# Attention with two feed-forward layers on one core: the high halves of k copied by GpSimd, and all pieces that prepare the next head pairs placed anew

## The chip, the core and the metric

The kernel runs on one core of one Trainium2 chip. Five engines run beside each other, each through its own instructions in a fixed order: TensorE (PE: matrix products and transposes, with its weight loads as PEld), VectorE (DVE), ScalarE (ACT), GpSimd (POOL), and SyncE (SP), which here only issues DMAs. ScalarE issues some DMAs too; these stand in its instruction order. Waits between engines go by semaphores. The metric is the device time of one execution in microseconds (us); lower is better.

## The reference

```python
q_pool = q.reshape(B, H, S // 2, 2, D).mean(axis=3)      # B=2, H=8, S=1152, D=64
scores = matmul(q_pool, k.T) / sqrt(D)                   # 576 x 1152 for each batch and head
attn = exp(scores - max(scores)); attn /= sum(attn) + 1e-9
x = matmul(attn, v)                                      # as 1152 tokens x 512
xn = x / sqrt(mean(x * x) + 1e-6) * rms_g
y = (silu(xn @ w_gate) * (xn @ w_val)) @ w_out           # 512 -> 1536 -> 512
h = y @ w_in2                                            # 512 -> 2048
out = (h * tanh(softplus(h))) @ w_out2                   # 2048 -> 512
```

All is float32. The kernel holds an operand of a product as a sum of two float16 numbers, a high half (the value rounded to float16) and a low half (what the rounding left), and adds the three products high-high, high-low and low-high.

## The kernel before

The 16 heads are worked on as 8 pairs of heads (the code's `g`, 0 to 7). A pair has 9 steps (its `j`): in each, 128 rows of pooled q of one head meet all 1152 keys; the last step of a pair takes 64 rows of both heads. So there are 72 steps, `n` from 0 to 71, and n mod 9 is called the step's place below, 0 to 8. The rest of the program (about 407 of the span's 657 us) is the feed-forward part.

`attn_step(n)` writes down the instructions of one step; they run in that order on each engine:

- TensorE: the scores of step n (six products of 128 x 384, tile `s` in PSUM; two buffers in turn); up to eight transposes of k and q halves for the next pair, where the step has them, into the first bank of the other score buffer; three transposes of the exponentials of step n-1 (tile `ep`, which has one buffer); the products of step n-5 with v (27 of them; 54 at the step that holds both heads).
- ScalarE: the high halves of the exponentials of step n-1 (`hl`, L296), those of the part transposed on TensorE (`et`, L323), a square for the RMS norm where one is due, a copy for the next pair where the plan has one (`kv_hi`, `q_hi`: tiles `khl`, `qhl`, `vv`), and the exponential of step n (`e`, L283), which needs the row maximum.
- VectorE: the row maximum of step n (L274), the copy of finished transposes to SBUF (`kqT`, L209), the low halves of `et` (L138), every few steps the division of finished rows of attention (`r`, `x`), and last the piece of `scale` that the plan has (`kv_scale`, `q_scale`: a multiplication by 64 in place, L145 and L174).
- GpSimd: the low halves of the exponentials of step n-1 (`hl`, L138: input minus high half), and the pieces of `pool` that the plan has (`kv_lo`, `q_add`, `q_lo`).

Before a pair begins, its k, q and v have to be loaded, multiplied by 64, split into halves and, for k and q, transposed. These pieces are spread over the steps of earlier pairs by the table `PLAN`: an entry (t, what) of an engine stands at step 9g + t for the pair g that it prepares. `FIRST` has other places for pair 1. `each(n, engine)` walks the table, and within a step the pieces of a smaller t's pair may come behind or ahead by the loop order.

A few buffers tie the pieces together. The loaded k and v lie in four buffers in turn (`nat`), so that a load waits for the low half of the tile that stood there; the halves of k (`khl`), those of q (`qhl`) and the sum of q's pairs (`qs`) have one buffer each; the exponentials (`e`) have three, the halves `hl` four, and `et` five. From step 42 the RMS norm of the first batch is worked in (every fourth step an `xn`, L537, on VectorE, with its halves `xh` on ScalarE and GpSimd), and from step 59 the first weight tiles (`gx`, `c`, `stretch`).

Of the kernel before, what the change touches and what calls it, by code (L numbers as in the profile page):

```python
# [41 lines left out]
def kernel(  # L42
# [13 lines left out]
    nc = tc.nc  # L56
    B, H, S, D = q.shape
# [15 lines left out]
    NTI = 2 * NI + 1  # L73
    NPR = B * NP
# [38 lines left out]
    nat, kqT, vvt, cvt = {}, {}, {}, {}  # L113
# [33 lines left out]
    def kv_hi(w, g, e):  # L147
        if e == 0:
            if w == "k":
                cvt["k", g] = cv_p.tile([128, 2 * NJ, 2 * D], F16, tag="khl", name="khl")  # L150
            else:
                t = kq_p.tile([128, 2 * NJ, 2 * D + 2], F16, tag="vv", name="vv")
                nc.gpsimd.memset(t[:, :, 2 * D:2 * D + 1], 1.0)
                vvt[g] = t
        t = (cvt["k", g] if w == "k" else vvt[g])[:, e * NJ:(e + 1) * NJ, :]
        o = 0 if w == "k" else D
        sc = 1.0 if g else QK_S if w == "k" else V_S
        nc.scalar.activation(out=t[:, :, o:o + D], in_=nat[w, g, e], func=ACTF.Copy, scale=sc)

    def kv_lo(w, g, e):  # L160
# [50 lines left out]
    def kq_first():  # L211

        t = kqT[0] = kq_p.tile([128, 2 * NJ + 2 * NTI, 128], F16, tag="kqT", name="kqT")
        for s0, n in ((2 * NJ, 2 * NTI), (0, 2 * NJ)):
            e = 0 if s0 else 1
            kv_hi("v", 0, e)
            kv_lo("v", 0, e)
            ps = s_buf[e].bitcast(F16)
            for s in range(s0, s0 + n):
                w, z = divmod(s - 2 * NJ, NTI)  # L220
                if s < 2 * NJ:
                    src = cvt["k", 0][:, s, :]
                else:
                    src = cvt["q", 0][:, z, w:w + 2, :].rearrange("p t d -> p (t d)")
                c, o = divmod(s - s0, 8)
                nc.tensor.transpose(out=ps[:, c, o * 128:(o + 1) * 128], in_=src, identity=ident)
            for c in range(-(-n // 8)):
                z = min(8, n - 8 * c)
                o = t[:, s0 + 8 * c:s0 + 8 * c + z, :]
                i = ps[:, c, 0:z * 128].rearrange("p (s t) -> p s t", s=z)  # L230
                if c == 1:
                    nc.vector.tensor_copy(out=o, in_=i)
                else:
                    nc.scalar.activation(out=o, in_=i, func=ACTF.Copy)
# [465 lines left out]
    def o_part(c, t, part, parts):  # L700
# [13 lines left out]
        if part == parts - 1:  # L714
            o = ot_p.tile([128, DM], F32, tag="ot", name="ot")
            nc.scalar.activation(out=o, in_=ps, func=ACTF.Copy, scale=1.0 / (G_S * W_S))
            for p0, p1, dst in out_rows(T):
# [4 lines left out]


    PLAN = {
        "load": [(-17, load, "k", 0), (-16, load, "k", 1), (-12, load, "q", 0), (-11, load, "q", 1), (-10, load, "q", 2),
                 (-9, load, "v", 0), (-5, load, "v", 1)],
        "act": [(-12, kv_hi, "k", 0), (-10, kv_hi, "k", 1), (-6, q_hi, 0), (-5, q_hi, 1), (-4, kv_hi, "v", 0),
                (1, kv_hi, "v", 1)],
        "scale": [(-13, kv_scale, "k", 0), (-11, kv_scale, "k", 1), (-7, q_scale), (-5, kv_scale, "v", 0),
                  (0, kv_scale, "v", 1)],  # L730
        "pool": [(-11, kv_lo, "k", 0), (-9, kv_lo, "k", 1), (-8, q_add), (-6, q_lo), (-3, kv_lo, "v", 0),
                 (2, kv_lo, "v", 1)],
        "flip": [(-9, 0), (-7, 1), (-4, 2), (-2, 3), (-1, 4)],
    }

    FIRST = {
        "load": {}, "act": {-12: -8, -10: -7}, "scale": {-13: -9, -11: -8}, "pool": {-11: -7, -9: -6},
        "flip": {-9: -6, -7: -5},
    }

    def each(n, engine):

        for t, *what in PLAN[engine]:
            for g in range(1, NPR):
                at = NTI * g + (FIRST[engine].get(t, t) if g == 1 else t)
                if at != n:
                    continue
                if engine == "flip":
                    yield g, FL[what[0]]
                else:  # L750
                    f, *a = what
                    f(*([a[0], g, a[1]] if f in (load, kv_hi, kv_lo, kv_scale) else [g, *a]))

    def do(n, engine):
        for _ in each(n, engine):
            pass

    def attn_step(n):
        scores(n)
        turns = list(each(n, "flip"))  # L760
        for g, f in turns:
            kq_flip(read[n - 1], g, *f)
        flip_pe(n - 1)
        split_hi(n - 1)
        if n:
            split_lo(n - 1)
            flip(n - 1)
        part_hi(n - 1)
        x_sums(1)
        do(n, "act")  # L770
        row_max(n)
        for g, f in turns:
            kq_keep(n - 1, g, f[0])
        part_lo(n - 1)
        row_exp(n)
        do(n, "pool")
        do(n, "load")
        if n >= LAG:
            attn_v(n - LAG)
            attn_r(n - LAG)  # L780
            attn_x(n - LAG)
        do(n, "scale")
        read.pop(n - 1, None)

    with tc.manual_schedule():
# [69 lines left out]
        for step in TAIL:  # L855
# [5 lines left out]
            else:  # L861
                n = NIT - LAG + int(step)
# [114 lines left out]
```

## Time and profile before

| | |
|---|---|
| Median of 3 runs | 658.35 us (657.65 to 659.39) |
| The profiled execution | 659.05 us, of which the span is 657.3 us |
| Steps 0 to 71 (first exponential to last) | 16.9 to 245.7 us |
| PE, DVE, ACT, POOL busy over the span | 91%, 63%, 60%, 47% |

The page of the profile gives busy time by engine and by line; the timelines give single instructions with their start and length, and in brackets how long the engine had been idle and what released it. A view by windows gives the busy time of each engine between two moments. An interval below is the time from one start of the exponential to the next: it is the length of a step on ScalarE.

### The profile page before, as it was taken

The numbers are of one execution on the slowest core, as the hardware profiler recorded it, in microseconds if no ns is written. First come the engines' busy times: TensorE is split into PE (matmuls) and PEld (weight loads), VectorE is DVE, ScalarE is ACT, GpSimd is POOL, SyncE is SP. The second block draws the span as 40 slices with busy tenths as digits, with TensorE's granted clock in tenths as the row PEclk, the third lists the DMA queues.
The fourth block names the chain that finished last, engine by engine and source line by source line (L and its number), as shares of the span: only waits on it lengthen the run. The fifth ranks groups of instructions, "written<-read, shape, count | busy, mean of one in ns | idle before, by whom it ended". The sixth has DMA issues, their size and how long they took to land.

```text
span 657.3 us, 14631 instructions
## 1 busy us (share of the span) xinstructions
PE 597.6 (91%) x5880; PEld 419.1 (64%) x5880; DVE 413.2 (63%) x679; ACT 391.7 (60%) x661; POOL 309.9 (47%) x255
## 2 busy tenths in 40 slices
PE   3588989887887789899999999999999999999997
PEld 2366767666656567677777777777655555555553
DVE  4798989889998896568888311554499931111110
ACT  4799999998987886666666331442455533223221
POOL 0778988878896861567778420441233310000000
PEclk9899999999998999999999999999999999999999
DMA  6599999998999996545556202453244100001001
GB/s 195 133 184 202 203 192 186 210 194 183 174 209 217 181 177 143 145 145 176 172 183 192 65 1 65 130 184 105 85 140 153 41 17 32 1 2 48 1 1 48
DMA packets 161908, 84.05 MB, mean 128 GB/s; under 512 B 124720, under 2 KB 152368, under 8 KB 161840
## 3 DMA queue, kind: packets, MB, share of 16 engines
q1 hardware_dynamic: 151184, 67.71, 46.8%
q10 hardware_dynamic: 10656, 15.40, 7.8%
q8 instruction: 46, 0.75, 0.5%
q14 instruction: 22, 0.18, 0.1%
HBM read 50.07 MB, written 2.36 MB: 80 GB/s over the span
## 4 chain that ended last, share of the span: by engine, by line
PE 65%; ACT 14%; DVE 8%; issue 8%; POOL 2%; ACTq 1%; DMA 1%; DVEq 0%; POOLq 0%
ACT e L283 6%; PE z L576 5%; PE z L578 5%; PE z L577 5%; PE po L713 5%; PE po L712 5%; PE po L711 5%; PE pg L576 3%; PE pv L578 3%; PE pg L577 3%; PE pv L576 3%; PE pv L577 3%; PE pg L578 3%; PE py L576 3%; PE py L578 3%
## 5 line engine op out<-in xcount | busy, mean ns | idle before, releaser
L138 POOL TENSOR_TENSOR hl<-e,hl 128x768 f16<-128x768 f32 x71 | 117.9, 1663 | 55.8 <-ACT hl L296 26.8
L274 DVE CUSTOM_DVE_ANT_1 junk<-s,shift 128x1152 bf16<-128x1152 f32 x72 | 97.2, 1351 | 8.1 <-PE s L255 7.5
L283 ACT ACTIVATE e<-s,m 128x1152 f32<-128x1152 f32 x72 | 87.6, 1217 | 13.6 <-DVE m L274 12.8
L255 PE MATMUL s<-kqT 128*128 128x384 f16 (+1 forms) x480 | 85.4, 333 | 10.2 <-DVE kqT L209 8.1
L140 DVE SCALAR_TENSOR_TENSOR g<-mo,g 128x384 f16<-128x384 f32 x48 | 26.8, 562 | 93.3 <-ACT g L686 93.3
L138 POOL TENSOR_TENSOR stretch<-c,stretch 128x512 f16<-128x512 f32 x40 | 47.8, 1194 | 60.6 <-ACT stretch L451 60.3
L347 PE MATMUL av<-vv,et 128*128 128x65 f16 (+1 forms) x720 | 74.1, 193 | 0.9 <-DVE x L395 0.9
L349 PE MATMUL av<-vv,et 128*128 128x64 f16 (+1 forms) x720 | 74.0, 193 | 0.0
L350 PE MATMUL av<-vv,et 128*128 128x65 f16 (+1 forms) x720 | 73.9, 195 | 0.0
L347 PEld LDWEIGHTS <-et 128*128 128x128 f16 (+1 forms) x720 | 67.2, 101 | 2.4 <-issue 2.3
L349 PEld LDWEIGHTS <-et 128*128 128x128 f16 (+1 forms) x720 | 67.0, 100 | 0.7
L350 PEld LDWEIGHTS <-et 128*128 128x128 f16 (+1 forms) x720 | 67.1, 100 | 0.0
L434 DVE TENSOR_SCALAR c<-raw 128x512 int32<-128x512 int32 x68 | 48.2, 708 | 26.6 <-POOL woh L138 24.5
L138 POOL TENSOR_TENSOR h<-fo,h 128x288 f16<-128x288 f32 x48 | 45.0, 937 | 42.0 <-ACT h L613 42.0
L296 ACT ACTIVATE hl<-e 128x768 f16<-128x768 f32 x72 | 60.6, 842 | 3.9 <-POOL khl L138 1.8
L576 PE MATMUL z<-y,w2i 128*128 128x384 f16 x192 | 62.6, 326 | 0.0
L577 PE MATMUL z<-y,w2i 128*128 128x384 f16 x192 | 62.6, 326 | 0.0
L578 PE MATMUL z<-y,w2i 128*128 128x384 f16 x192 | 62.6, 326 | 0.0
L680 ACT ACTIVATE mo<-z 128x384 f32<-128x384 f32 x48 | 23.2, 484 | 64.1 <-PE z L578 63.9
L444 DVE SCALAR_TENSOR_TENSOR c<-gx,c 128x512 int32<-128x512 int32 x52 | 57.7, 1110 | 4.1 <-ACT gx L424 2.2
L255 PEld LDWEIGHTS <-kqT 128*128 128x128 f16 (+1 forms) x480 | 39.7, 101 | 31.7 <-issue 13.5
L576 PE MATMUL pg<-stretch 128*128 128x288 f16 x192 | 54.9, 286 | 2.1 <-DMA stretch<-xh 1.6
(110 smaller groups left out, 1549.1 us busy)
## 6 DMA issues: line engine op xcount, KB each, us to landing
raw<-in_moe_w_out_dram SPq DMA_DIRECT2D x28, 512.0 KB, 3.4
raw<-in_moe_w_in_dram SPq DMA_DIRECT2D x16, 512.0 KB, 3.9
raw<-in_moe_w_gate_dram SPq DMA_DIRECT2D x8, 512.0 KB, 3.5
raw<-in_moe_w_val_dram SPq DMA_DIRECT2D x8, 512.0 KB, 3.8
vn<-in_v_dram ACTq DMA_DIRECT2D x14, 288.0 KB, 4.4
kn<-in_k_dram ACTq DMA_DIRECT2D x12, 288.0 KB, 4.1
qn<-in_q_dram ACTq DMA_DIRECT2D x12, 256.0 KB, 3.8
raw<-in_moe_w_gate_dram ACTq DMA_DIRECT2D x4, 512.0 KB, 4.7
```

Of the source, the lines that this page charges most:

```text
L138: eng.tensor_tensor(out=out_, in0=in_, in1=hi, op=ALU.subtract)
L255: mm = nc.tensor.matmul(out=ps[p0:p0 + m, c, 0:SN], lhsT=qt[:, w * NTI + slot, p0:p0 + m], rhs=kt[:, e * NJ + c * per:e * NJ + (c + 1) * p ...
L274: nc.vector.tensor_tensor_reduce(out=junk.rearrange("p (c s) -> p c s", c=SC), in0=ps[:, :, 0:SN], in1=shift.unsqueeze(2).to_broadcast([12 ...
L283: nc.scalar.activation(out=e.rearrange("p (c s) -> p c s", c=SC), in_=ps[:, :, 0:SN], func=ACTF.Exp, bias=m, scale=s_scale)
L296: nc.scalar.activation(out=t[:, 0, :], in_=e_t[n][:, 0:NB * 128], func=ACTF.Copy)
L347: nc.tensor.matmul(out=av[0:m, o0:o0 + D + 1], lhsT=hi, rhs=vr[:, D:2 * D + 1], start=(jj == 0), stop=False)
L349: nc.tensor.matmul(out=av[0:m, o0:o0 + D], lhsT=hi, rhs=vr[:, 0:D], start=False, stop=False)
L350: nc.tensor.matmul(out=av[0:m, o0:o0 + D + 1], lhsT=et[:, z + (NB if jj < NB else PB), p0:p0 + m], rhs=vr[:, D:2 * D + 1], start=False, st ...
L444: nc.vector.scalar_tensor_tensor(out=c, in0=g, scalar=3, in1=c, op0=ALU.logical_shift_left, op1=ALU.bitwise_or)
L576: nc.tensor.matmul(out=ps, lhsT=w0, rhs=x0, start=(i == 0), stop=False)
L577: nc.tensor.matmul(out=ps, lhsT=w0, rhs=x1, start=False, stop=False)
L578: nc.tensor.matmul(out=ps, lhsT=w1, rhs=x0, start=False, stop=(i == n - 1))
```

## The change

The high halves of k for the pairs 2 to 7 are copied by `tensor_copy` on GpSimd instead of an activation on ScalarE; pairs 0 and 1 keep ScalarE. The plan is written anew: k is loaded, multiplied and split one step earlier, the pieces on ScalarE are left with q at t = -6 and -4 and v at -2 and 1, both low halves of v stand within their own pair at t = 1 and 2, and the multiplication of v's first half moves from t = -5 to -3. The transposes stay. `FIRST` becomes a full table for pair 1.

```diff
         o = 0 if w == "k" else D
         sc = 1.0 if g else QK_S if w == "k" else V_S
+        if w == "k" and g > 1:
+            nc.gpsimd.tensor_copy(out=t[:, :, o:o + D], in_=nat[w, g, e])
+            return
         nc.scalar.activation(out=t[:, :, o:o + D], in_=nat[w, g, e], func=ACTF.Copy, scale=sc)
...
     PLAN = {
-        "load": [(-17, load, "k", 0), (-16, load, "k", 1), (-12, load, "q", 0), (-11, load, "q", 1), (-10, load, "q", 2),
-                 (-9, load, "v", 0), (-5, load, "v", 1)],
-        "act": [(-12, kv_hi, "k", 0), (-10, kv_hi, "k", 1), (-6, q_hi, 0), (-5, q_hi, 1), (-4, kv_hi, "v", 0),
-                (1, kv_hi, "v", 1)],
-        "scale": [(-13, kv_scale, "k", 0), (-11, kv_scale, "k", 1), (-7, q_scale), (-5, kv_scale, "v", 0),
+        "load": [(-18, load, "k", 0), (-17, load, "k", 1), (-14, load, "q", 0), (-13, load, "q", 1), (-12, load, "q", 2),
+                 (-7, load, "v", 0), (-6, load, "v", 1)],
+        "act": [(-6, q_hi, 0), (-4, q_hi, 1), (-2, kv_hi, "v", 0), (1, kv_hi, "v", 1)],
+        "scale": [(-14, kv_scale, "k", 0), (-12, kv_scale, "k", 1), (-8, q_scale), (-3, kv_scale, "v", 0),
                   (0, kv_scale, "v", 1)],
-        "pool": [(-11, kv_lo, "k", 0), (-9, kv_lo, "k", 1), (-8, q_add), (-6, q_lo), (-3, kv_lo, "v", 0),
-                 (2, kv_lo, "v", 1)],
+        "pool": [(-13, kv_hi, "k", 0), (-12, kv_lo, "k", 0), (-11, kv_hi, "k", 1), (-10, kv_lo, "k", 1), (-9, q_add),
+                 (-6, q_lo), (1, kv_lo, "v", 0), (2, kv_lo, "v", 1)],
         "flip": [(-9, 0), (-7, 1), (-4, 2), (-2, 3), (-1, 4)],
     }
-    FIRST = {
-        "load": {}, "act": {-12: -8, -10: -7}, "scale": {-13: -9, -11: -8}, "pool": {-11: -7, -9: -6},
-        "flip": {-9: -6, -7: -5},
-    }
+    FIRST = dict(
+        PLAN,
+        act=[(-8, kv_hi, "k", 0), (-7, kv_hi, "k", 1), (-5, q_hi, 0)] + PLAN["act"][1:],
+        scale=[(-9, kv_scale, "k", 0), (-8, kv_scale, "k", 1), (-7, q_scale)] + PLAN["scale"][3:],
+        pool=[(-9, q_add), (-7, kv_lo, "k", 0), (-6, kv_lo, "k", 1), (-5, q_lo)] + PLAN["pool"][6:],
+        flip=[(-6, 0), (-5, 1)] + PLAN["flip"][2:],
+    )
     def each(n, engine):
-        for t, *what in PLAN[engine]:
-            for g in range(1, NPR):
-                at = NTI * g + (FIRST[engine].get(t, t) if g == 1 else t)
-                if at != n:
+        for g in range(1, NPR):
+            for t, *what in (PLAN if g > 1 else FIRST)[engine]:
+                if NTI * g + t != n:
                     continue
```

Three places show the order before and now. The first is VectorE in steps 14 to 16 (places 5 to 7), before; `junk, m` is the row maximum that opens a step, `kn` a loaded half of k multiplied by 64.

```order
L209 COPY kqT<-s 128x1024
L138 TENSOR_TENSOR et<-ep,et 128x384
L145 TENSOR_SCALAR kn<-kn 128x2x288
L274 ISA junk,m<-s,shift 128x1152
L274 ISA m 128x1
L138 TENSOR_TENSOR et<-ep,et 128x384
```

The same stretch of VectorE now, from the copy of step 14 to the row maximum of step 16; `vn` is the first half of v of pair 2, `kn` the second half of k of pair 3.

```order
L212 COPY kqT<-s 128x1024
L138 TENSOR_TENSOR et<-ep,et 128x384
L277 ISA junk,m<-s,shift 128x1152
L277 ISA m 128x1
L138 TENSOR_TENSOR et<-ep,et 128x384
L145 TENSOR_SCALAR vn<-vn 128x2x288
L145 TENSOR_SCALAR kn<-kn 128x2x288
L277 ISA junk,m<-s,shift 128x1152
```

Before, place 5 ended in one multiplication and place 6 in none; now place 5 has none and place 6 has two in a row, and the next row maximum stands behind both. This is so at place 6 of each of the pairs 0 to 5.

The second place is GpSimd in steps 13 to 18, before: the low halves of the exponentials, and between them the constant column of v (`MEMSET`) and the low halves of v and k.

```order
L138 TENSOR_TENSOR hl<-e,hl 128x768 x2
L153 MEMSET vv 128x18
L138 TENSOR_TENSOR hl<-e,hl 128x768
L138 TENSOR_TENSOR vv<-vn,vv 128x9x64
L138 TENSOR_TENSOR hl<-e,hl 128x768
L138 TENSOR_TENSOR khl<-kn,khl 128x9x64
L138 TENSOR_TENSOR hl<-e,hl 128x768 x2
L138 TENSOR_TENSOR khl<-kn,khl 128x9x64
```

GpSimd in the same steps now; `CAST` is the copy of k's high half.

```order
L138 TENSOR_TENSOR hl<-e,hl 128x768 x2
L159 CAST khl<-kn 128x9x64
L138 TENSOR_TENSOR hl<-e,hl 128x768
L138 TENSOR_TENSOR khl<-kn,khl 128x9x64
L138 TENSOR_TENSOR hl<-e,hl 128x768
L153 MEMSET vv 128x18
L159 CAST khl<-kn 128x9x64
L138 TENSOR_TENSOR hl<-e,hl 128x768
L138 TENSOR_TENSOR khl<-kn,khl 128x9x64
```

At place 6 (step 15) the low half of k's first tile now follows that of the exponentials; before, it was the low half of v. Each step from place 5 round to place 3 now has a piece on GpSimd beside the low half of the exponentials, and place 4 has none.

The third place is VectorE where the RMS norm is worked in, in step 54 (place 0) of the kernel now; `xn` is the normalised row, L540 there.

```order
L212 COPY kqT<-s 128x1024
L138 TENSOR_TENSOR et<-ep,et 128x384
L145 TENSOR_SCALAR vn<-vn 128x2x288
L540 SCALAR_TENSOR_TENSOR xn<-x,w_2312,gbc 128x512
L277 ISA junk,m<-s,shift 128x1152
```

That stretch reads alike before; of the other steps with an `xn`, step 50 before had a multiplication of k in front of it and step 58 one of v, both of which are gone from there now, while step 46 now has that of q.

## Rows read from the trace of the kernel before

**Rows 1.** Windows (pairs 0, 2, 6): length; busy of PE, PEld, DVE, ACT, POOL; PEclk; DMA.
```profile
16.93:46.90 29.97, 21.46 (x258) 15.14 (x259) 24.71 (x41) 25.62 (x34) 21.66 (x16) 0.89 0.77 154
...
73.88:100.64 26.76, 23.89 (x400) 18.43 (x397) 24.36 (x47) 25.24 (x34) 22.90 (x17) 1.00 1.10 201
...
186.11:219.93 33.82, 26.05 (x401) 19.70 (x397) 31.09 (x50) 26.59 (x36) 25.99 (x19) 0.95 0.97 199
```

**Rows 2.** Timeline of ScalarE, pair 2: start, length, line, tiles, [idle before, released by].
```profile
76.83 1.21 ACT L283 ACTIVATE e<-s,m 128x1152 f32<-128x1152 f32 x1
...
82.63 1.22 ACT L283 ACTIVATE e<-s,m 128x1152 f32<-128x1152 f32 x1
...
88.18 0.49 ACT L323 ACTIVATE et<-ep 128x384 f16<-128x384 f32 x1 [0.51 <-PE ep L318]
...
89.14 1.21 ACT L283 ACTIVATE e<-s,m 128x1152 f32<-128x1152 f32 x1
90.39 0.85 ACT L296 ACTIVATE hl<-e 128x768 f16<-128x768 f32 x1
91.14 0.47 ACT L323 ACTIVATE et<-ep 128x384 f16<-128x384 f32 x1
91.51 0.67 ACT L158 ACTIVATE khl<-kn 128x576 f16<-128x576 f32 x1
...
92.08 1.21 ACT L283 ACTIVATE e<-s,m 128x1152 f32<-128x1152 f32 x1
...
94.71 1.22 ACT L283 ACTIVATE e<-s,m 128x1152 f32<-128x1152 f32 x1
...
97.86 1.21 ACT L283 ACTIVATE e<-s,m 128x1152 f32<-128x1152 f32 x1
...
100.64 1.22 ACT L283 ACTIVATE e<-s,m 128x1152 f32<-128x1152 f32 x1
```

**Rows 3.** Timeline of GpSimd, steps 24 and 25.
```profile
91.37 1.65 POOL L138 TENSOR_TENSOR hl<-e,hl 128x768 f16<-128x768 f32 x1 [1.85 <-issue]
...
94.30 1.65 POOL L138 TENSOR_TENSOR hl<-e,hl 128x768 f16<-128x768 f32 x1
```

**Rows 4.** Timeline of VectorE, steps 23 to 26.
```profile
89.75 0.45 DVE L145 TENSOR_SCALAR kn<-kn 128x576 f32<-128x576 f32 x1
...
95.32 0.95 DVE L145 TENSOR_SCALAR kn<-kn 128x576 f32<-128x576 f32 x1
96.25 1.36 DVE L274 CUSTOM_DVE_ANT_1 junk<-s,shift 128x1152 bf16<-128x1152 f32 x1
...
99.17 1.36 DVE L274 CUSTOM_DVE_ANT_1 junk<-s,shift 128x1152 bf16<-128x1152 f32 x1
```

**Rows 5.** Timeline of VectorE, step 54.
```profile
187.00 0.60 DVE L145 TENSOR_SCALAR vn<-vn 128x576 f32<-128x576 f32 x1
187.52 1.77 DVE L537 SCALAR_TENSOR_TENSOR xn<-x,w,gbc 128x512 f32<-128x512 f32 x1
```

**Rows 6.** Timeline of GpSimd, steps 54 and 55.
```profile
187.25 1.49 POOL L138 TENSOR_TENSOR khl<-kn,khl 128x576 f16<-128x576 f32 x1
188.71 2.08 POOL L138 TENSOR_TENSOR hl<-e,hl 128x768 f16<-128x768 f32 x1
```

**Rows 7.** Timeline of ScalarE, steps 58 and 59.
```profile
199.48 1.21 ACT L283 ACTIVATE e<-s,m 128x1152 f32<-128x1152 f32 x1
...
205.63 1.22 ACT L283 ACTIVATE e<-s,m 128x1152 f32<-128x1152 f32 x1 [2.48 <-DVE m L274]
```

**Rows 8.** Timeline of VectorE, step 58.
```profile
200.81 1.40 DVE L145 TENSOR_SCALAR vn<-vn 128x576 f32<-128x576 f32 x1
202.13 2.13 DVE L537 SCALAR_TENSOR_TENSOR xn<-x,w,gbc 128x512 f32<-128x512 f32 x1
```

**Rows 9.** Instructions on tile khl: count, ns min/median/max, first and last start.
```profile
L138 POOL TENSOR_TENSOR khl<-kn,khl x14: 1279/1505/1512, 23.9 to 187.2; 128x576 f16<-128x576 f32 x14
```

**Rows 10.** Groups of GpSimd: busy us, mean ns, idle before.
```profile
masks.py:199 POOL TENSOR_SCALAR_AFFINE_SELECT ident<-ident 128x128 f16<-128x128 f16 x1 | 0.3, 295 | 0.1
```

## The prediction, made before the kernel ran

> **What bounds the kernel now.** I read the windows of the attention part by pairs first, then the timelines of ScalarE, VectorE and GpSimd over one pair, since a table of places can only be judged step by step. In pair 2, which has nothing but attention in it, four engines are nearly full: of 26.76 us ScalarE is busy 25.24, VectorE 24.36, TensorE 23.89 and GpSimd 22.90 [rows 1]. So the reader should not look for the one engine that bounds, but at each place for the last wait. ScalarE alone sets the least length of a step: from an exponential's start to that of `hl` 1.25 us (90.39 less 89.14), to `et` 0.75 more, to the next piece 0.37, together 2.37; a copy for the next pair adds 0.57 (92.08 less 91.51) [rows 2].
>
> Two waits lengthen that. One is TensorE's: at place 4 `et` waited 0.51 us for the transposes behind the products of the step with both heads [rows 2]. The other is between VectorE and GpSimd. A multiplication on VectorE takes 0.45 us while GpSimd rests, but 0.95 when it starts at 95.32 while GpSimd's low half of 94.30 runs until 95.95: it ends 0.32 after that [rows 3, 4]. Two such operations in a row are worse. In step 54 `vn` was directly followed by `xn` on VectorE; GpSimd's next instruction started in between (187.25), and `xn` took 1.77 us, ending 0.55 after GpSimd's end at 188.74 [rows 5, 6]. In step 58 the same couple took 1.40 and 2.13, and the exponential waited 2.48 us for its row maximum in an interval of 6.15 us [rows 7, 8]. The second of two such operations waits for a whole instruction of GpSimd.
>
> **The change part by part**, for a pair of the middle (intervals by place, before from [rows 2]).
>
> Place 5 loses k's copy on ScalarE: 2.94 becomes 2.37, -0.57. Place 7 loses the other: 3.15 becomes about 2.6, -0.55. With ScalarE shorter, place 8 is left with VectorE's own work, 2.92 from one row maximum to the next (96.25 to 99.17 [rows 4]) against 2.78 before, +0.14. Places 3 and 4 together took 6.51 (82.63 to 89.14); a q copy leaves place 4, but TensorE's chain through 54 products stands there, so 0. Place 0 keeps 2.95.
>
> Places 1 and 2 took 5.80 (76.83 to 82.63). q's multiplication moves from place 2 to place 1, where it meets GpSimd's low half again: that runs until about 1.5 after the exponential's start (below), the multiplication ends 0.32 later, the row maximum starts 0.08 before that, and the exponential 1.45 after the row maximum (from 99.17 to 100.64 it was 1.47 [rows 2, 4]): about 3.2. Place 2 has a q copy and 2.37 + 0.57 = 2.94. Sum 6.1, +0.3.
>
> Place 6 is where two multiplications now stand in a row, with nothing between them. GpSimd's low half starts 0.13 after `hl` ends (91.37 against 91.24) and lasts 1.65 [rows 2, 3], so it ends 1.25 + 0.85 + 0.13 + 1.65 = 3.88 after the exponential of place 5, which is 1.51 after that of place 6. The first multiplication arrives within it and ends at 1.51 + 0.32 = 1.83. GpSimd's next instruction, k's low half, is ready (its high half was made a step before) and goes in between: 1.28 undisturbed [rows 9], 1.49 with a VectorE operation ahead of it [rows 6], from 1.47 to 2.96. The second multiplication ends at 3.28, the row maximum starts at 3.20, the exponential at 4.65. Before it was 2.63: +2.0. Queued behind the second multiplication on VectorE are that row maximum, and behind it the exponential, everything on ScalarE, and TensorE's transposes.
>
> One pair: -0.57 - 0.55 + 0.14 + 0.3 + 2.0 = +1.3 us; pairs 1 to 3 make +3.9.
>
> The new instruction, the copy on GpSimd, is not in the trace. Below it is a one-input operation of 128 elements at 0.295 us [rows 10], above it the two-input operation of its own shape at 1.28 [rows 9]. I take 0.9, nearer to the latter. At place 5 it lies in a gap (GpSimd sat idle 1.85 us before 91.37 [rows 3]), and no multiplication stands in place 5 or 7; only in the steps with norms would 1.3 instead of 0.9 show, with +0.8 in all.
>
> There one may weigh a rule that speaks against the change. The Trainium skill (Perfetto Trace Analysis, Optimizing Scalar/DVE Operations) reminds that GpSimd reads SBUF by a port of VectorE's, so that work put on one may hold up the other. By that rule twelve copies of 0.9 would take up to 11 us out of VectorE; by the places none meets a VectorE multiplication, and the sum takes nothing for it. No run here shows the copy yet.
>
> Pair 0: place 6 with +2.0, places 5, 7 and 8 with -1.0, and q's low half one step later behind a low half of the exponentials, for which transposes wait, +0.5. The loads of v now wait on ScalarE for k's low halves in steps 2 and 3 (before, one load of k did), and `hl` queues behind each; TensorE's transposes wait for the same low halves, so I add nothing. Together +1.5, between +0.5 and +3. Pairs 4 and 5: squares on ScalarE already lengthen places 3 and 5, so GpSimd's low half ends earlier against the exponential and place 6 costs about 1.4; with the copies gone from ScalarE the rest nearly pays for it: +0.2 each. Pair 6: step 58 loses its `vn` in front of `xn`, and 6.15 [rows 7] becomes place 4's usual 3.6 (6.51 less some 2.9 for place 3) plus 1.0 for an `xn` that waits once, 4.6: -1.55. v's multiplication stands in step 60 instead, in front of an operation on the first weights, +1.4 as in pairs 4 and 5; step 61 gains about 1.3, the length of v's low half (the shape of [rows 9]), which GpSimd has no longer in front of it; place 3 gains 0.57, places 0 to 2 lose 0.3. Sum about -1.8; these are estimates. Pair 7: +0.1.
>
> All: 1.5 + 3.9 + 0.4 - 1.8 + 0.1 = +4.1 us, on a path that ends with the attention part; the feed-forward part behind it starts later by as much and is not changed. The profiled execution took 659.05 us and would take 663.15; the median of the runs lies 0.7 below that execution, so 658.35 + 4.1 = 662.4 us.
>
> **The rivals.** First, VectorE may start its second multiplication before GpSimd's waiting instruction gets in; the two of place 6 then cost 0.37 more (0.45 less the 0.08 of overlap), the place is 3.5 instead of 4.65, and in pairs 0 to 4 that takes off about 1.1 each. 4.1 - 5.5 = -1.4: 657.0 us, not slower. For it: the two rows of before have an `xn`, another operation, second. Against it: GpSimd's instruction stands ready in both, and got in both times. It decides from the length of the second `kn` at place 6: 0.4 or 1.5.
>
> The Trainium skill (SBUF — State Buffer, Who interferes with whom) has a rule for just this: the pair of ports common to VectorE and GpSimd is locked by the instruction that issues first, for its whole length, whichever engine that is. Issue order would give this rival if VectorE's second operation came first; by the rows GpSimd's came first, and the trace agrees with the rule (1.77 and 2.13 us for the second).
>
> Second, the granted clock. It was 0.89 over pair 0, where TensorE waits for the first k and q, and 0.95 over pair 6 with its long interval, and 1.00 in pair 2 [rows 1]; 0.05 of 33.82 us is 1.7 us of clock lost, as 3.4 us at the lower of the two levels (1.2 instead of 2.4 GHz) would lose it. The hole of 2.0 us at place 6 comes six times; if the clock falls each time and half of it reaches the path, that is +5: 667.4 us. Against it: pair 6, with an interval of 6.15 us [rows 7], shows no more than that.
>
> Third, ScalarE, the fullest engine of pair 2, may be the bound after all: twelve copies of 0.57 leave it, 6.8 us, and if the longer waits on VectorE lie beside TensorE's products the kernel takes 651.5 us. Against it: VectorE has 24.36 of 26.76 us already, and its waits come out of that remainder.
>
> **How the numbers follow.** Forecast 0.63, first rival 0.17, second 0.12, third 0.08. I count a difference of over 0.3% (2.0 us) as told apart from no change. Slower: all but a little of the forecast and the second rival, 0.74. Within 0.3%: most of the first rival and the low edge of the forecast, 0.14. Faster: the third and a quarter of the first, 0.12. The forecast's own range is 660 to 665, from pair 0's bounds, the copy's, and +1.0 to +1.5 for a middle pair. The whole range is 656.8 to 667.0: it holds the first rival and nearly the second, and leaves out the third.
>
> **What would show it.** Right: in steps 6, 15, 24, 33, 42 and 51 `vn` at about 1.2 us and `kn` behind it at about 1.5, GpSimd's k low half between, and an exponential that waits over 1 us for its row maximum; a pair 2 of about 28.0 us; intervals of 2.4 at places 3 and 5; step 58 near 4.6. Wrong: `kn` at 0.45 behind `vn`; copies on GpSimd over 1.3 us that push its low halves into later steps; a granted clock below 1.00 in pairs 1 to 5; or a feed-forward part of another length than before.

## The result: 9.4 us slower, more than twice the forecast

The changed kernel took 668.3 us (median of 4 runs, 666.88 to 668.68), the kernel before 658.87 us (4 runs, 657.65 to 660.75): the ratio is 1.0141, 95% interval 1.0117 to 1.0165. The forecast was 662.4 us with 667.0 as its upper end. The sign was right, and so was the wait that it named. Two losses that it had not counted make up most of the rest: one operation of VectorE that GpSimd held up in pair 7, and stretches at the lower level of TensorE's clock.

**The profile after.** The profiled execution took 668.59 us with a span of 666.8 us, 9.5 us more than before. The feed-forward part behind the last exponential is as long as it was: 255.25 to 666.8 us is 411.5 us, and before 245.71 to 657.3 was 411.6. So all of it lies in the attention part. First the windows of pairs 0, 2, 6 and 7 and of single steps (17, 56, 15 and 66; columns as in [rows 1]; pair 7 to the start of its last exponential).

```profile
17.27:48.75 31.48, 23.01 (x263) 15.90 (x262) 25.63 (x41) 24.89 (x32) 21.82 (x17) 0.86 0.78 148
78.21:105.89 27.68, 24.18 (x407) 18.82 (x404) 25.35 (x47) 24.22 (x32) 22.91 (x19) 1.00 1.06 186
193.25:225.93 32.68, 26.14 (x401) 19.84 (x397) 28.74 (x50) 26.81 (x36) 24.50 (x18) 0.95 1.14 211
225.93:255.25 29.32, 22.36 (x365) 16.69 (x363) 24.64 (x42) 22.93 (x32) 20.16 (x14) 0.94 0.99 158
74.17:78.21 4.04, 4.04 (x48) 3.02 (x46) 2.88 (x8) 2.45 (x4) 4.04 (x4) 0.62 0.75 153
201.11:205.22 4.11, 4.11 (x54) 2.96 (x52) 2.44 (x5) 3.13 (x5) 4.11 (x4) 0.71 1.16 301
...
66.60:71.58 4.98, 3.78 (x61) 2.81 (x58) 4.85 (x6) 3.00 (x5) 4.78 (x3) 1.00 1.22 265
...
235.41:241.72 6.31, 3.76 (x65) 2.60 (x63) 6.09 (x8) 2.45 (x5) 4.66 (x4) 1.00 1.10 157
```

The same stretch of pair 7 in the kernel before:

```profile
219.93:245.71 25.78, 20.41 (x363) 15.68 (x362) 22.39 (x42) 22.82 (x32) 18.82 (x13) 1.00 1.05 188
```

Pair 2 has grown from 26.76 to 27.68 us at the full clock, with ScalarE 1.02 us less busy and VectorE 0.99 more. Pair 7, which the forecast passed over with +0.1, has grown by 3.54 and has a granted clock of 0.94 where it was 1.00. Step 17, at 74.17 us, took 4.04 us at a clock of 0.62, with TensorE busy for all of it.

Place by place, from the starts of the exponentials (us):

| place | 0 | 1 | 2 | 3 | 4 | 5 | 6 | 7 | 8 | pair |
|---|---|---|---|---|---|---|---|---|---|---|
| pair 2 before | 2.95 | 2.63 | 3.17 | 2.95 | 3.56 | 2.94 | 2.63 | 3.15 | 2.78 | 26.76 |
| pair 2 after | 3.08 | 2.64 | 2.94 | 2.36 | 4.13 | 2.36 | 4.65 | 2.58 | 2.93 | 27.68 |
| pair 1 after | 2.95 | 3.09 | 2.94 | 2.36 | 4.14 | 2.36 | 4.99 | 2.58 | 4.04 | 29.45 |
| pair 6 after | 4.86 | 3.01 | 4.10 | 2.48 | 4.03 | 3.29 | 4.51 | 2.94 | 3.46 | 32.68 |
| pair 7 after | 3.38 | 2.79 | 3.31 | 6.30 | 2.92 | 4.82 | 2.38 | 3.42 | | |
| pair 7 before | 3.37 | 3.08 | 3.32 | 3.21 | 3.10 | 3.92 | 2.54 | 3.24 | | |

**Place 6** is as forecast. Timeline of VectorE in step 24 (columns as in [rows 2]):

```profile
96.34 1.23 DVE L145 TENSOR_SCALAR vn<-vn 128x576 f32<-128x576 f32 x1
97.49 1.53 DVE L145 TENSOR_SCALAR kn<-kn 128x576 f32<-128x576 f32 x1
98.94 1.34 DVE L277 CUSTOM_DVE_ANT_1 junk<-s,shift 128x1152 bf16<-128x1152 f32 x1
```

GpSimd at the same time, and then ScalarE:

```profile
95.59 1.65 POOL L138 TENSOR_TENSOR hl<-e,hl 128x768 f16<-128x768 f32 x1 [1.88 <-issue]
97.19 1.51 POOL L138 TENSOR_TENSOR khl<-kn,khl 128x576 f16<-128x576 f32 x1
98.66 1.85 POOL L138 TENSOR_TENSOR hl<-e,hl 128x768 f16<-128x768 f32 x1
```

```profile
95.73 1.22 ACT L286 ACTIVATE e<-s,m 128x1152 f32<-128x1152 f32 x1
...
100.38 1.22 ACT L286 ACTIVATE e<-s,m 128x1152 f32<-128x1152 f32 x1 [1.35 <-DVE m L277]
```

Read the three together: `vn` ends at 97.57, 0.33 behind the end of `hl` (97.24); GpSimd's low half of k has already started at 97.19, so `kn` lasts 1.53 and ends 0.32 behind it; the row maximum starts behind `kn`, and ScalarE waits 1.35 us for it. The single multiplication that stood a place earlier took 0.45 [rows 4].

The new copy on GpSimd, from the view of the tile `khl`:

```profile
L159 POOL CAST khl<-kn x12: 659/662/669, 35.9 to 188.3; 128x576 f16<-128x576 f32 x12
```

0.66 us, below the 0.9 that was assumed between [rows 9, 10].

**Step 66** (place 3 of pair 7) is the first loss that was not counted. VectorE, GpSimd and ScalarE there:

```profile
236.77 3.58 DVE L437 TENSOR_SCALAR c<-raw 128x512 int32<-128x512 int32 x1
240.27 1.34 DVE L277 CUSTOM_DVE_ANT_1 junk<-s,shift 128x1152 bf16<-128x1152 f32 x1
```

```profile
230.14 1.70 POOL L138 TENSOR_TENSOR vv<-vn,vv 128x576 f16<-128x576 f32 x1
...
234.52 1.23 POOL L138 TENSOR_TENSOR vv<-vn,vv 128x576 f16<-128x576 f32 x1
235.71 1.15 POOL L138 TENSOR_TENSOR stretch<-c,stretch 128x512 f16<-128x512 f32 x1
236.83 3.24 POOL L138 TENSOR_TENSOR hl<-e,hl 128x768 f16<-128x768 f32 x2
```

```profile
235.41 1.22 ACT L286 ACTIVATE e<-s,m 128x1152 f32<-128x1152 f32 x1
236.67 0.84 ACT L299 ACTIVATE hl<-e 128x768 f16<-128x768 f32 x1
...
241.72 1.22 ACT L286 ACTIVATE e<-s,m 128x1152 f32<-128x1152 f32 x1 [3.83 <-DVE m L277]
```

`c<-raw`, the first operation on a weight tile, takes 0.41 us when nothing holds it. Here it lasted 3.58: it ended 0.28 us behind the second of two low halves that GpSimd ran one straight behind the other (236.83 to 240.07). It came at 236.77, before either of them started; the second could not start before ScalarE had made its high half at 237.51 (236.67 and 0.84). GpSimd was late because the new plan puts v's first low half into step 64, where before it had been made in step 60.

### The profile page after: what moved, and what is told of

Read it like the earlier page. It is cut to its first block, busy times and chain, and to the rows that moved or that the text cites. A ratio compares the mean times of both kernels' runs of the same rounds, so it can differ in the third digit from the quotient of the medians.

```text
span 666.8 us, 14631 instructions
## 1 busy us (share of the span) xinstructions
PE 605.0 (91%) x5880; PEld 423.0 (63%) x5880; DVE 419.9 (63%) x679; ACT 386.0 (58%) x649; POOL 316.5 (47%) x267
## 3 DMA queue, kind: packets, MB, share of 16 engines
HBM read 50.07 MB, written 2.36 MB: 79 GB/s over the span
## 4 chain that ended last, share of the span: by engine, by line
PE 57%; ACT 2%; DVE 2%; issue 1%; POOL 0%; DMA 0%; ACTq 0%; DVEq 0%
PE z L579 5%; PE z L581 5%; PE z L580 5%; PE po L716 5%; PE po L715 5%; PE po L714 5%; PE pg L579 3%; PE pg L580 3%; PE pv L581 3%; PE pv L580 3%; PE pv L579 3%; PE pg L581 3%; PE py L579 3%; PE py L581 3%; PE py L580 3%
## 5 line engine op out<-in xcount | busy, mean ns | idle before, releaser
L258 PE MATMUL s<-kqT 128*128 128x384 f16 (+1 forms) x480 | 90.9, 344 | 13.3 <-DVE kqT L212 10.9
L350 PE MATMUL av<-vv,et 128*128 128x65 f16 (+1 forms) x720 | 75.3, 195 | 0.9 <-DVE x L398 0.9
L353 PE MATMUL av<-vv,et 128*128 128x65 f16 (+1 forms) x720 | 75.0, 196 | 0.0
L350 PEld LDWEIGHTS <-et 128*128 128x128 f16 (+1 forms) x720 | 68.0, 102 | 2.6 <-issue 2.5
L352 PEld LDWEIGHTS <-et 128*128 128x128 f16 (+1 forms) x720 | 67.9, 101 | 0.8
L353 PEld LDWEIGHTS <-et 128*128 128x128 f16 (+1 forms) x720 | 68.0, 101 | 0.0
L437 DVE TENSOR_SCALAR c<-raw 128x512 int32<-128x512 int32 x68 | 50.3, 740 | 26.5 <-POOL woh L138 24.4
```

The costliest lines, as they stand in the source:

```text
L258: mm = nc.tensor.matmul(out=ps[p0:p0 + m, c, 0:SN], lhsT=qt[:, w * NTI + slot, p0:p0 + m], rhs=kt[:, e * NJ + c * per:e * NJ + (c + 1) * p ...
L350: nc.tensor.matmul(out=av[0:m, o0:o0 + D + 1], lhsT=hi, rhs=vr[:, D:2 * D + 1], start=(jj == 0), stop=False)
L352: nc.tensor.matmul(out=av[0:m, o0:o0 + D], lhsT=hi, rhs=vr[:, 0:D], start=False, stop=False)
L353: nc.tensor.matmul(out=av[0:m, o0:o0 + D + 1], lhsT=et[:, z + (NB if jj < NB else PB), p0:p0 + m], rhs=vr[:, D:2 * D + 1], start=False, st ...
```

## The experiments

Theories. T1: the time goes where an operation of VectorE waits for GpSimd's instructions. T2: the granted clock falls behind the holes this makes, and costs more. T3: the copies on GpSimd cost the time.

### One multiplication moved off place 6

```diff
-        "scale": [..., (-3, kv_scale, "v", 0),
+        "scale": [..., (-4, kv_scale, "v", 0),
```

> The new kernel with one entry changed: the multiplication of v's first half stands at t = -4 (place 5) instead of -3 (place 6), so that place 6 has one multiplication on VectorE and place 5 one. Theory T1 (the second of two multiplications in a row waits for a whole instruction of GpSimd): the intervals of place 6, 4.6 to 5.0 us in pairs 0 to 3 and 4.0 to 4.5 in pairs 4 to 6, fall to about 3.2; place 5 stays within 0.3 of 2.4, since GpSimd is between two instructions there; in step 50 an xn now follows the multiplication and one waits more. In all -8 to -10 us, from 668.3 to 658 to 660.5. Theory T2 (the granted clock falls behind the holes of place 6 and costs as much again): the stretches at the lower level from 73.8 and 172.8 us are gone as well, step 17 goes from 4.04 back to about 2.9, and the total is 656 to 658. Theory T3 (the copies on GpSimd cost the time, by the port that VectorE shares): place 6 shortens, but the time comes back in other places, 665 to 668.

Measured: 661.17 us (660.02 to 661.66), ratio to the kernel before 1.0034 (1.0017 to 1.005). VectorE from place 5 to 6 of pair 2:

```profile
90.42 0.45 DVE L145 TENSOR_SCALAR vn<-vn 128x576 f32<-128x576 f32 x1
...
92.78 1.21 DVE L145 TENSOR_SCALAR kn<-kn 128x576 f32<-128x576 f32 x1
```

Both lengths as T1 has them: `vn` is free at place 5, `kn` waits once. Place 6 of pair 3 fell from 4.65 to 3.21, place 5 stayed at 2.43. In pairs 1 and 5 place 6 fell only to 4.2 and 3.9, and the total lies 0.7 above T1's range. The one entry gives back 7.1 of the 9.4 us. T3 alone is out: the copies were all kept. Step 17 went back to 2.87, and the stretches at the lower clock in pairs 1 and 5 are gone, while those in steps 56 and 68 stayed and `c<-raw` of step 66 still lasted 3.58. This does not show T2: the five runs on step 66 below, whose pairs 0 to 6 are those of the changed kernel, have no such stretch in pairs 1 and 5 either.

### v's old places for pair 7 alone

```diff
+    LAST: as PLAN, but v's pieces at load -9, -5; scale -5, 0; act -4, 1; pool -3, 2
-            for t, *what in (PLAN if g > 1 else FIRST)[engine]:
+            for t, *what in (LAST if g == NPR - 1 else PLAN if g > 1 else FIRST)[engine]:
```

> The new kernel with v's places of the kernel before for pair 7 alone (load -9 and -5, multiplication -5 and 0, high half -4 and 1, low half -3 and 2). Theory T1 (c<-raw of step 66 lasted 3.58 us because GpSimd ran v's two low halves of steps 64 and 65 and so had a queue of ready instructions): c<-raw falls to 0.4 to 1.2 us, step 66 from 6.30 to about 3.3, step 60 from 4.51 to about 3.3; in all -4 to -4.5, from 668.3 to about 664. With T2 (the clock that fell at 244.5 us fell because of that hole) step 68 goes from 4.82 to about 3.9 as well: 663. Rival (c<-raw waited for its weights or for a buffer, not for GpSimd): it stays at 3.6 us, only step 60 shortens: about 667.

Measured: 665.3 us (665.08 to 665.67), ratio 1.0104 (1.0088 to 1.0121). VectorE, then GpSimd, around step 66:

```profile
237.12 0.79 DVE L437 TENSOR_SCALAR c<-raw 128x512 int32<-128x512 int32 x1
```

```profile
235.99 1.64 POOL L138 TENSOR_TENSOR hl<-e,hl 128x768 f16<-128x768 f32 x1
238.00 1.65 POOL L138 TENSOR_TENSOR hl<-e,hl 128x768 f16<-128x768 f32 x1 [0.36 <-ACT hl L299]
```

With one vv less in its queue GpSimd is on time; the second `hl` is not ready when the first ends. Step 66 fell to 3.80, and step 68 to 3.92. T1 held, and 3.0 us came back, 2.4 by the two ratios (4 to 5 were expected; step 61 gave 1.4 away again).

### The copy alone, in the kernel before

```diff
+        if w == "k" and g > 1:
+            nc.gpsimd.tensor_copy(out=t[:, :, o:o + D], in_=nat[w, g, e])
+            return
         nc.scalar.activation(out=t[:, :, o:o + D], in_=nat[w, g, e], func=ACTF.Copy, scale=sc)
```

> The kernel before with one edit: the high halves of k of the pairs 2 to 7 are copied by GpSimd instead of ScalarE, in the same steps; every other piece keeps its old place. T1: ScalarE loses 0.57 us at places 6 and 8, the copy of 0.66 us on GpSimd meets no multiplication, nothing doubles: faster than 658.9 by 0.5 to 1.0 in each of six pairs, 653 to 656. T3 (a copy on GpSimd holds VectorE up by its 0.66 us, or delays the low half of the exponentials behind it): slower, 12 times 0.3 to 0.7: 662 to 667. If what ScalarE gains is not on the path: 658 to 660.

Measured: 662.87 us (662.12 to 663.15), ratio 1.0065 (1.005 to 1.008). T1's number was a miss: it is 4.2 us slower. GpSimd in pair 2, then VectorE:

```profile
93.58 1.65 POOL L138 TENSOR_TENSOR hl<-e,hl 128x768 f16<-128x768 f32 x1 [1.86 <-issue]
95.17 0.67 POOL L159 CAST khl<-kn 128x576 f16<-128x576 f32 x1
95.79 1.25 POOL L138 TENSOR_TENSOR vv<-vn,vv 128x576 f16<-128x576 f32 x1
97.00 1.66 POOL L138 TENSOR_TENSOR hl<-e,hl 128x768 f16<-128x768 f32 x1
```

```profile
97.36 1.62 DVE L145 TENSOR_SCALAR kn<-kn 128x576 f32<-128x576 f32 x1
```

No VectorE multiplication stands beside the copy. But the copy sets the next low half of the exponentials back: it starts 3.42 us behind the one before it (93.58 to 97.00), where it was 2.93 (91.37 to 94.30 [rows 3]), and `kn`, with the shorter step, comes 0.17 sooner. So `kn` now comes 0.36 us into that low half, not 1.02 [rows 3, 4], and waits for nearly all of it: 1.62 instead of 0.95. Step 25 went from 3.15 to 3.87, step 27 (with a `vn`) from 2.95 to 3.82, against -0.51 at place 5. T3 has part of this right, by way of the low half behind the copy. With the old places the copy is a loss; in the new plan, with `vn` moved and the copies kept, the kernel is faster than this one.

### The low half of k moved away from place 6

```diff
-        (-12, kv_lo, "k", 0), (-11, kv_hi, "k", 1)
+        (-11, kv_lo, "k", 0), (-11, kv_hi, "k", 1)
```

> The new kernel with one entry changed: the low half of k's first tile stands at t = -11 (place 7, in front of the second copy) instead of -12 (place 6), so that the two multiplications of place 6 stay in a row but GpSimd has no instruction ready behind the low half of the exponentials. T1 (GpSimd's ready instruction gets in between): kn at place 6 falls from 1.53 to about 0.5 us and the place from 4.65 to about 3.6; GpSimd then has 3.6 us of work at place 7 against a step of 2.6, and half of the gain is lost again there: 662 to 666. Rival (two multiplications in a row take that long by themselves): kn stays at 1.5 us, place 6 at 4.65, and the total is 668 to 671.

Measured: 665.89 us (662.96 to 667.04), ratio 1.0106 (1.0078 to 1.0133). VectorE in step 24:

```profile
92.70 1.21 DVE L145 TENSOR_SCALAR vn<-vn 128x576 f32<-128x576 f32 x1
93.83 0.45 DVE L145 TENSOR_SCALAR kn<-kn 128x576 f32<-128x576 f32 x1
```

The two multiplications still stand in a row. With nothing ready on GpSimd behind `hl`, the second takes 0.45 and place 6 is 3.56: it is GpSimd's instruction between them that costs the 1.1 us. The runs of this kernel lie 4 us apart; why is not shown, since only one of them has a trace.

### Five runs on step 66

What keeps `c<-raw` out for two instructions, when `kn` at place 6 was kept out for one? T1a: the moment at which it comes (T1a' in two expectations: some 0.2 us around the start of GpSimd's instruction). T1b: the two `hl` standing ready. T1c: the operation itself. All five runs are the changed kernel with an edit at step 66.

```diff
+        if part == 0 and job is jobs[2]:
+            nc.vector.memset(c[:, 0, 0:64], 0)      # first run; second run: all of c
```

> The new kernel with one tiny instruction added: VectorE clears 128x64 elements of c (some 0.1 us) in front of c<-raw of step 66, so that c<-raw starts some 0.1 us later, behind the start of GpSimd's first hl instead of 0.06 in front of it. Theory T1a (c<-raw lost twice because it started just in the change from one instruction of GpSimd to the next): it now waits for one low half alone, 1.6 + 0.3 = about 1.9 us instead of 3.58, step 66 goes from 6.30 to about 4.7, and the total from 668.3 to 666.5. Theory T1b (a queue of GpSimd instructions that are all ready keeps VectorE out at whatever moment it comes): c<-raw still lasts about 3.5 us, no change. Rival (c<-raw waits for its data): it ends at the same moment as before, no change.

> The new kernel, with VectorE clearing all of c (128x512, some 0.4 to 0.6 us) in front of c<-raw of step 66, so that c<-raw comes about 0.6 us into GpSimd's first hl, as the multiplications come into theirs. Theory T1a' (an operation that comes within some 0.2 us of the start of GpSimd's instruction loses to the next one too): it now gets in between the two hl, ends 0.3 us after the first, about 1.3 us long, and step 66 goes from 6.30 to about 4.7. Theory T1b (two hl that both stand ready keep VectorE out at any moment): c<-raw ends 0.28 us after the second hl again, about 2.8 us long, and step 66 stays at 6.3.

Measured: 667.96 us (667.0 to 670.55; ratio 1.0148, 1.011 to 1.0185), and 669.64 in one execution. VectorE in the second:

```profile
236.89 0.48 DVE L437 MEMSET c<- 128x512 int32 x1
237.41 2.90 DVE L439 TENSOR_SCALAR c<-raw 128x512 int32<-128x512 int32 x1
```

In both it ended 0.28 us behind the second `hl` again (first run: from 236.38, 0.14 us behind the start of the first `hl`, for 3.38 us). T1a falls.

```diff
+        if n == 67:
+            nc.gpsimd.memset(pad, 0.0)
         if n:
             split_lo(n - 1)
```

> The new kernel, with a tiny instruction on GpSimd (128x18 elements cleared, 0.17 us as the one in front of v's halves) between the two hl at which c<-raw of step 66 waits. T1b (it is the change from one hl straight to the next, with both ready, that keeps VectorE out): c<-raw gets in at the tiny instruction and ends about 0.3 to 0.5 us after the first hl, 2.0 to 2.2 us long instead of 3.58; step 66 goes to about 4.8. T1a' (the moment at which c<-raw comes): it is the same as in the new kernel, so c<-raw stays out of the second hl's time too and lasts 3.6 to 3.8 us.

Measured: 668.73 us in one execution. GpSimd, then VectorE:

```profile
235.87 1.64 POOL L139 TENSOR_TENSOR hl<-e,hl 128x768 f16<-128x768 f32 x1
237.45 0.11 POOL L771 MEMSET pad<- 128x18 f32 x1
237.52 1.63 POOL L139 TENSOR_TENSOR hl<-e,hl 128x768 f16<-128x768 f32 x1
```

```profile
235.83 3.61 DVE L438 TENSOR_SCALAR c<-raw 128x512 int32<-128x512 int32 x1
```

An instruction between the two `hl` does not let it in. Then another operation in its place, with `c<-raw` one step later:

```diff
+            nc.vector.memset(c, 0)
+            # first run: c (as float) * 1; second run: c >> 29, c read in place of raw
+            return
```

> The run with all of c cleared first, but in step 66 a float multiplication of c by 1 in place (VectorE, as the multiplications of k and v) stands where c<-raw stood, and c<-raw follows one step later, directly in front of c<-gx. T1b (two hl that stand ready keep any such operation of VectorE out): the multiplication lasts 2.9 us and ends 0.3 us after the second hl. T1c (it lies in c<-raw itself, an integer shift that reads every second word): the multiplication gets in between the two hl, as vn does at place 6, and ends 0.32 us after the first, 1.3 us long; step 66 goes from 6.29 to about 4.7.

> The same, but in step 66 VectorE shifts c itself (128x512 integers that lie together) where c<-raw shifted every second word of raw. T1b: 2.9 us, to 0.3 us after the second hl. T1c, if it lies in the reading of raw: it gets in between, 1.3 us long. T1c, if it lies in the integer shift: 2.9 us again, while the multiplication of the run before this one gets in.

Measured: 668.55 and 667.75 us in one execution each. VectorE in the first, then in the second:

```profile
237.48 2.92 DVE L439 TENSOR_SCALAR c<-c 128x512 f32<-128x512 f32 x1
```

```profile
236.59 2.92 DVE L438 TENSOR_SCALAR c<-c 128x512 int32<-128x512 int32 x1
```

A float multiplication is held as long as the shift, so T1c falls as well; neither of the two reads the weights, so it is not a wait for these. T1b is left, but the kernel before speaks against it as it stands. There too two `hl` ran one straight behind the other, in step 49 (GpSimd, then VectorE):

```profile
170.55 3.46 POOL L138 TENSOR_TENSOR hl<-e,hl 128x768 f16<-128x768 f32 x2
```

```profile
171.31 1.20 DVE L145 TENSOR_SCALAR vn<-vn 128x576 f32<-128x576 f32 x1
```

The high half for the second was done at 172.06, before the first ended at 172.19, and `vn` still got in between: it ended at 172.51, 0.32 behind the first, and the two `hl` took 3.46 us instead of 3.24. So two `hl` that stand ready do not by themselves keep VectorE out. What is shown is that the wait of step 66 goes when the second `hl` is not ready at the end of the first (second experiment). What lets VectorE in at place 6 and in step 49, and not here, stays open.

### Towards a better version

```diff
 # all three: vn at -4, and for pair 7 v's first copy at -3, its low half at -2
-        (-8, q_scale)              # second and third run
+        (-7, q_scale)
-        (-12, kv_scale, "k", 1)    # third run
+        (-13, kv_scale, "k", 1)
```

> The new kernel with two edits: v's first multiplication at t = -4 as in the run with only that edit (661.2 us, with the copies on GpSimd kept), and for pair 7 alone v's first half copied at -3 and its low half made at -2 (step 61) instead of 1 (step 64), so that GpSimd has no queue of ready instructions at step 66. T1: step 66 falls from 6.31 to 3.2 to 3.8, the stretch at the lower clock behind it goes, nothing else moves: 661.2 - 2.5 to -3.8 = 657.4 to 658.7. Rival (the wait of step 66 has another cause, or moves on to the next such operation): 660 to 661.

> The kernel of the run before it, with q's multiplication at t = -7 (place 2) again instead of -8 (place 1) for the pairs 2 to 7. T1 (the multiplication at place 1 waits 1.5 us since the low half that it meets started only 0.4 before it; at place 2 it meets one further on): places 1 and 2 go from 6.13 together to about 5.85 in five pairs, -1 to -1.5: 656 to 657.5. Rival (the wait is the same at either place): no change.

> The kernel of the run before it, with k's second multiplication at t = -13 (place 5, in a row with v's) instead of -12 (place 6). T1 (what a multiplication costs is whether GpSimd runs at that moment, and at place 5 GpSimd lies between two instructions): both take 0.45 to 0.6 us there, place 5 goes from 2.43 to about 2.9 and place 6 from 3.2 to 3.4 down to 2.65: -0.1 to -0.3 a pair, 655 to 657. Rival (two multiplications in a row are bad wherever they stand): place 5 goes to 4.5, and the total to 664 or more.

Measured: 658.57 us (656.35 to 663.65; ratio 1.0009, 0.9984 to 1.0034), 657.24 us (655.09 to 659.1; 0.9972, 0.9955 to 0.9988) and 658.19 us (656.63 to 659.53; 0.9981, 0.9967 to 0.9996). In the first, step 66 fell to 3.79, and in its profiled execution, the fastest of the ten, no stretch of pairs 1 to 7 stood at the lower clock. In the second, places 1 and 2 of pair 3 went from 6.11 to 5.91 (5.85 expected). In the third the two multiplications stand in a row at place 5, where GpSimd lies between two instructions, and take 0.45 each, as T1 has it. But place 5 of pair 3 rose from 2.43 to 2.80 and place 6 stayed at 3.21, since ScalarE's own pieces and TensorE's transposes fill it there, so nothing was gained (655 to 657 were expected). The second of the three is some 1.8 us faster than the kernel before; it has the lowest median of all, but is not told apart from the third.

## Why the forecast was wrong

**Place 6, +2.0 a pair: right.** Measured +2.02 in pairs 2 and 3, with `vn` 1.23 and `kn` 1.53 against 1.2 and 1.5; the experiments with `vn` and with k's low half moved show that this couple and the instruction between its halves cause it. The first rival (the second multiplication gets in first) is out.

**The other places: right.** Places 3 and 4 together 0, place 5 -0.58, place 7 -0.57, place 8 +0.15, as forecast; places 1 and 2 gave -0.2 to +0.2 where +0.3 stood. A middle pair came to +0.9 and +1.1 (pairs 2 and 3) against +1.3. Pair 0 came to +1.51 against +1.5, at a granted clock of 0.86 where it had been 0.89, so that part of this agreement is luck. Pairs 4 and 5 came to +0.16 and +0.64 against +0.2 each.

**The copy at nothing: right only in its places.** It took 0.66 us and met no multiplication at places 5 and 7. Put into the old plan it costs 4.2 us. The Trainium skill (Perfetto Trace Analysis, Optimizing Scalar/DVE Operations) warns that work moved between GpSimd and VectorE might not help, for the port that they share. That run bears the warning out by a detour, for this work came from ScalarE and the copy itself met no VectorE multiplication: the low half behind it came later, at 97.00 us, and held `kn` for 1.62.

**Pair 7, +0.1: this step failed.** It measured +3.54, of which step 66 has 3.09 and step 68 0.90; in the five runs on step 66 it was +3.4 to +4.6. The prediction judged the places of a middle pair and looked at the weights' operations only where `vn` stands in front of one (step 60). It did not write down GpSimd's queue for steps 62 to 66, where v's two low halves, a norm's and a weight's low half now stand in a row, and VectorE's next operation on the weights behind them.

**The clock, a rival at 0.12 and +5 us: a part of it came.** In pairs 1 to 7 four steps of the profiled execution stood in a stretch at 1.2 GHz: 17, 48, 56 and 68. Step 17 took 4.04 us at a granted clock of 0.62; in the run with v's old places for pair 7, which is the same program up to there, and in the first run on step 66 it took 2.93 at 1.00. Windows of that run:

```profile
75.21:78.14 2.93, 2.87 (x53) 2.36 (x50) 2.84 (x8) 2.56 (x4) 2.93 (x3) 1.00 0.90 198
201.26:204.21 2.95, 2.72 (x40) 1.88 (x38) 2.78 (x5) 2.92 (x5) 2.95 (x3) 1.00 1.14 305
```

The second row is step 56, which took 4.10 us at 0.71 in the changed kernel, in its stretch from 200.1 us. So these two lost 1.11 and 1.15; step 68 lost 0.90 (at 0.66, against v's old places at 1.00) and step 48 0.40 (2.77, against 2.37 in the first run on step 66): 3.6 us in the four steps. Not all of it stayed. Pairs 1 to 6 together took 177.2 us, and 175.6 in the first run on step 66, which has none of the first three stretches: 1.6 us and not 2.7, since later steps were shorter in turn. Step 58 took 4.03 behind the slow step 56, and 4.57 without it. So the clock has some 2.5 of the 9.5 us.

Each fall came behind a hole: TensorE was busy 3.78 of 4.98 us in step 15, 3.09 of 4.57 in step 46, 3.42 of 4.86 in step 54 and 3.76 of 6.31 in step 66. But the first run on step 66 had the same hole in step 15 (3.77 of 4.99) and no fall behind it. Of the six holes at place 6, to which the rival gave its 5 us, only that of step 15 was followed by a fall, in this one execution. Behind step 66 the clock fell in all eight traces in which that step took 6.3 us. The forecast's own sign of being wrong, a clock below 1.00 in pairs 1 to 5, did come, in pairs 1 and 5. So a hole makes a fall possible, not certain, and the fall that came each time hangs on the step that the forecast had not looked at. How much clock is in the other three executions of the median is not known; their mean granted clocks do not order their times (668.0 us at 0.992, 666.88 at 0.989).

**The sum.** 9.5 us = 3.1 (step 66) + 2.5 (the clock) + 3.9 for all the rest, where the forecast had 4.1. The rest includes +0.34 at the start, which is not the change's: the first exponential started between 16.87 and 18.41 us in the traces of these kernels. In the first run on step 66, whose pairs 1 to 6 are free of the lower clock, pairs 0 to 6 came to +4.0 us, as forecast (pairs 1 to 3 +1.36, +1.24 and +1.07; pair 6 -1.46 against -1.8, with step 58 at 4.57 against 4.6). The other traces with the same pairs 0 to 6 have +4.4 to +5.7, so the agreement to a tenth is luck; that the terms of these pairs were right is not.

## What to carry to other kernels

Before work is moved onto GpSimd, write GpSimd's queue and VectorE's list beside each other for every step of the program, the odd ones at its end too, and ask at which moment of a running GpSimd instruction each VectorE operation comes; a piece that costs nothing itself can shift that moment. At place 6 here, the second of two such operations in a row cost a whole GpSimd instruction where one was ready behind the running one, and 0.45 us where none was. A long hole on TensorE can bring a fall of the clock: the four steps that stood in one took 0.4 to 1.15 us more, of which later steps gave a part back. Such a share belongs into the sum with its chance, not beside it as a rival.

## What was not expected of the hardware

An operation of VectorE can be kept out by two GpSimd instructions in a row, in step 66 for 2.9 to 3.6 us, with each of the operations and moments that were tried; in step 49 of the kernel before it was let in between two such instructions, and what decides is open. The Trainium skill (SBUF — State Buffer, Who interferes with whom) says that the pair of ports common to VectorE and GpSimd goes to the instruction that issues first, for its whole length. By that rule one may expect `c<-raw`, which stood waiting from 236.77 us, to come before the second `hl`, which was ready at 237.51; the trace has the second `hl` first, and the measurement decides. At place 6 the trace agrees with the rule.
